# Batch 0's first values as floats over SyncE, cast by ScalarE

## The chip, the cores and the metric

The kernel runs on one core of one Trainium2 chip. Five engines work beside each other, each through its own instructions in program order, and wait for each other by semaphores: TensorE (PE), VectorE (DVE), ScalarE (ACT), GpSimd (POOL) and SyncE (SP). Sixteen DMA engines move data between the chip's main memory and its on-chip memory. DMAs are issued from SP and ACT on hardware queues (q1 in the profile is SP's) and from POOL on a software queue (q0). A DMA from POOL can change float32 to bfloat16 on its way; here those from SP carry the values as they are.

The metric is the device time of one execution, in microseconds (us), as the median of several runs.

## The reference

Two chained attentions feed a two-layer network. The 8 batches have 8 heads each, with 576 rows of 64 for q, k and v, and 32 "packing" rows p:

```python
def sm_attn(qq, kk, vv):
    s = scale * np.matmul(qq, kk.transpose(0, 1, 3, 2))
    s = s - np.max(s, axis=-1, keepdims=True)
    a = np.exp(s)
    a = a / (np.sum(a, axis=-1, keepdims=True) + 1e-09)
    return np.matmul(a, vv)
p_packed = sm_attn(p, k, v)
out = sm_attn(q, p_packed, p_packed)
```

The result, as 4608 rows of 512, goes through `h = x @ w_in` (512 by 2048), `g = relu(h) ** 2` and `g @ w_out` (2048 by 512). All inputs and the output are float32; the kernel computes in bfloat16 with float32 sums.

## The kernel before

**Order.** All instructions are issued by the class `Kernel` from one long string, `ORDER` (line 48). Each word is one step, `step` (line 780) turns it into a call, and a suffix names the engine (`:a` ACT, `:v` DVE, `:p` POOL). Nothing reorders the steps: every engine does its share of the words in the order of the string. The semaphore waits between engines come from the tiles that the steps write and read. So the place of a word decides what stands behind it on its engine.

**Work.** Heads are taken in "quads" of four (`QH`), two quads to a batch. For each batch the kernel loads k (`Lk`), v (`Lv`) and q (`Lq`, or `LA` and `LB` for two pieces), computes the first attention (scores `s1`, maximum `m1`, exponential `x1`, turning `eT` and its copy `eo`, product with the values `pv`), normalizes (`rd`, `pp`), and then the second attention from `zA`/`zB` or `s2` on. The second attention's weights are not multiplied with the packed values on their own: `w0` to `w3` multiply the packed values into `w_in`, so that layer 1 (`h`, then `r` for the relu and `q` for the square) works from the attention weights. Layer 2 is `o`, and `c` and `d` copy and store its rows. Digits after a word are batch and quad, or tile numbers. While batch 0's attention runs, there is nothing else for PE but `Z` words: matmuls on zeros (`busy`, line 337) whose result is not used.

**The start.** These words begin the string:

```python
pf Lk00 P0 Lk01 kT00 Z14.0 s100 Lv00 LA0 kT01 m100 Z1.1 s101 m101 I x100 Lv01 x101 P1 Z2.1 eT00 LB0 eo00:v Z0.1 eT01
```

- `pf` (`p_first`, line 226) issues three DMAs on SP: batch 0's p and the first quad of batch 1 (96 KB), then the rest in two pieces (24 KB and 8 KB). They land as floats in `p_f`, a corner of the tile `gT` that is not yet in use.
- `P0` (`p_cast`, line 232) has DVE scale and cast the two quads of batch 0 (line 235) and transpose them to `pT` (line 239). `P1` does so for batch 1. The scores need `pT`.
- `Lk00` and `Lk01` (line 297 on) load the two quads of keys from POOL, `Lv00` and `Lv01` (`load_v`, line 305) the two quads of values, `LA0` and `LB0` the queries, `Wi` pieces of `w_in`. They all share POOL's queue, in the order of the words. `I` makes the identity matrix on POOL.
- `kT00` and `kT01` (`st_k`, line 354) have DVE transpose the keys when they have landed. `s100` and `s101` (line 411) are the scores on PE, `Z14.0` fourteen fillers ahead of them and `Z1.1` two between them.
- `m100`, `m101` are DVE's maxima, `x100`, `x101` ACT's exponentials (line 451). They are ACT's first work.

For batches 0 and 1 a quad of values lies as 96 partitions by 4 heads by 6 rows of 64 in bfloat16, in a row of `gT` for each quad that is not yet in use; batch 0's first quad lies in row 14 and batch 1's quads in rows 12 and 11. `pv` (line 488) reads it from there, about 12 us into the span.

A DMA's packets are the contiguous rows that it moves: a quad of keys has 128 rows of 18 x 64 floats, a quad of values 96 x 4 rows of 6 x 64 floats, the first load of p 128 x 3 rows of 64 floats.

Of the kernel before, what the change touches and what calls it, by code (L numbers as in the profile page):

```python
# [11 lines left out]
F32 = mybir.dt.float32  # L12
# [9 lines left out]
D = 64  # L22
NP = 32
T = 18
S = T * NP
HALF = S // 2
QH = 4
# [18 lines left out]


ORDER = """
pf Lk00 P0 Lk01 kT00 Z14.0 s100 Lv00 LA0 kT01 m100 Z1.1 s101 m101 I x100 Lv01 x101 P1 Z2.1 eT00 LB0 eo00:v Z0.1 eT01
QA01 QA00 eo01:v Wi01 EA00:a rd0 pv0 pp0 EA01:a Z1.0 pt0 Wi00 po0:v Z0.1 zA0 tA00 Wi11 tA01 mA00 Z1.0 QB01 QB00 EB00:a  # L50
EB01:a mA01 sA00:v Wi10 Wi20 Z2.1 zB0 sA01:v xA00 xA01 tB00 Z5.0 w00 tB01 Wi21 mB00 W001:a Z3.0 w10 uA01 uA00 mB01
sB00:p aA01:p xB00 W000:a TA01 sB01:v aA00:p TA00 Lk11 uB00 W100:a h0.0.2 h0.0.3 Lk10 h0.0.0 xB01 h0.0.1 W101:a r0.0.3:a
# [82 lines left out]
class Kernel:  # L135
# [83 lines left out]
    def bank(self, pool, name):  # L219

        return self.banks(pool).tile([P, 512], F32, name=name, tag="t")

    def packed(self, g0, g1):
        return self.p.rearrange("b (q h) i d -> (h i) (b q) d", h=QH)[:, g0:g1, :]

# [65 lines left out]
    def load1(self, b, qd, n):  # L291
# [10 lines left out]
        else:  # L302
            self.load_rows(x, s, qd if b else 0)

    def load_v(self, t, s, b, qd):

        if b in THREES:
            c = b * S
            x = self.gT[:, self.NFB - 2 - 2 * b - qd, c:c + QH * 6 * D].rearrange("p (h j d) -> p h j d", h=QH, d=D)[:S // 6]
            t["v"] = [x[:, :, j, :] for j in range(6)]  # L310
            self.nc.gpsimd.dma_start(x, s.rearrange("h (p j) d -> p h j d", j=6))
            return
        x = self.v_b[self.loaded_v % len(self.v_b)]
        self.loaded_v += 1
        y = self.v_end[b % len(self.v_end)]
        t["v"] = [x[:, :, j, :] for j in range(4)]
        t["v_end"] = y
        o, r = (D, 0) if qd else (0, 4 * P)
        self.nc.gpsimd.dma_start(x, s[:, o:o + 4 * P].rearrange("h (p j) d -> p h j d", j=4))  # L319
        self.nc.gpsimd.dma_start(y[qd * D:(qd + 1) * D, :, qd, :], s[:, r:r + D].rearrange("h p d -> p h d"))  # L320
# [459 lines left out]
    def step(self, word):  # L780
        word, _, e = word.partition(":")
        engine = self.engines.get(e, self.nc.vector)
        q4 = self.NFB // 4
        if word == "I":
            make_identity(self.nc, self.ident)
        elif word == "pf":
            self.p_first()
        elif word in ("Pr", "Px", "Pt", "Pu"):
            self.p_rest(word, engine)
        elif word in ("P0", "P1"):  # L790
            self.p_cast(int(word[1]))
        elif word[0] == "Z":
            self.busy(*map(int, word[1:].split(".")))
        elif word[:2] == "Wi":
            self.load_w_in(int(word[2]), int(word[3]))
        elif word[:2] == "Wo":
            self.load_w_out(int(word[2]) * q4, (int(word[2]) + 1) * q4)
        elif word[:2] in ("w0", "w1", "w2", "w3"):
            self.st_wp(int(word[2]), int(word[1]))
        elif word[:2] in ("W0", "W1", "W2", "W3"):  # L800
            self.st_wp_out(int(word[2]), int(word[1]), engine, *map(int, word[3:]))
        elif word[:2] in ("s1", "s2", "zA", "zB", "rd", "pv", "pp", "bd", "bs", "pt", "po"):
            self.step_quads(word[:2], engine, int(word[2]), *([int(word[3])] if len(word) > 3 else range(self.NQ)))
        elif word[0] == "L" and len(word) == 3:
            self.load_q(int(word[2]), {"q": None, "A": 0, "B": 1}[word[1]])
        elif word[0] == "L":
            self.load1(int(word[2]), int(word[3]), word[1])
        elif "." in word or word[0] in "cd":
            {"H": self.step_hh, "R": self.step_rr, "h": self.step_h, "r": self.step_r, "q": self.step_q, "o": self.step_o, "c": self.step_c, "d": self.step_d}[word[0]](
                engine, *map(int, word[1:].split(".")))  # L810
        else:
            self.step_att(word[:-2], engine, int(word[-2]), int(word[-1]))
# [56 lines left out]
```

## Time and profile before

| | before |
|---|---|
| time, median of 3 runs | 240.65 us (240.53 to 240.82) |
| profiled execution | 240.85 us |
| its span, first to last instruction | 239.1 us |
| PE busy | 230.8 us, 97% of the span |
| DVE busy | 200.4 us, 84% |
| ACT busy | 143.9 us, 60% |
| POOL busy | 73.0 us, 31% |
| chain that ended last | PE 92%, DVE 5%, ACT 1% |
| POOL's queue q0 | 25312 packets, 18.55 MB, 53.7% of 16 engines' span |
| SP's queue q1 | 6384 packets, 9.51 MB, 14.9% |

How to read it: busy times count instructions that compute; the issue of a DMA and semaphore waits are not counted for PE, DVE and ACT. The chain that ended last is followed back from the last instruction to what released each step, so it says which engine's work set the end. "Idle before" in a row is the time for which the engine stood still just before an instruction, and behind the arrow is what ended that. The lines of the DMA queues give packets, megabytes and the time that the packets took as a share of all 16 engines over the stretch asked for; packets that overlap in time count twice, so shares over 100% occur. Megabytes are those written: a cast load reads twice as many.

### The profile page before, as it was taken

To read this page: it belongs to the slowest core of one execution; us is meant where nothing else is said; L and a number is where in the kernel's file an instruction comes from. 1 tells how busy PE (TensorE), PEld (TensorE's weight loads), DVE (VectorE), ACT (ScalarE), POOL (GpSimd) and SP (SyncE) were. 2 spreads that over 40 slices of the span, in tenths; PEclk is the share of its full clock that TensorE was granted. 3 is DMA by queue.
4 is the path that set the end of the run, shared out by engine and by line. 5 is a ranking of instruction groups with operands and counts; after the bars stand their busy time and mean duration, and the time that the engine had idled before them with its cause. 6 is when DMAs were issued, how large, how long until landed. Compare 5 with 4: busy or idle time off the path is not lost.

```text
span 239.1 us, 5971 instructions
## 1 busy us (share of the span) xinstructions
PE 230.8 (97%) x2355; PEld 123.5 (52%) x2355; DVE 200.4 (84%) x455; ACT 143.9 (60%) x311; POOL 73.0 (31%) x122
## 2 busy tenths in 40 slices
PE   8887999999999999999999999999999999999994
PEld 2444553456544564456545654565545644555543
DVE  2779986998997889989998889997899789987740
ACT  2348974887896657775683648774485346732300
POOL 8509782785664661054203340002000000000000
PEclk9999999999999999999999999999999999999999
DMA  6999999999999979169923993216112112111224
GB/s 109 193 200 213 200 206 204 161 243 211 199 203 217 192 106 143 44 91 197 127 64 45 195 129 60 47 44 96 45 27 67 47 44 46 44 47 44 49 59 111
DMA packets 31868, 28.50 MB, mean 119 GB/s; under 512 B 8161, under 2 KB 26337, under 8 KB 31841
## 3 DMA queue, kind: packets, MB, share of 16 engines
q0 software_dynamic: 25312, 18.55, 53.7%
q1 hardware_dynamic: 6384, 9.51, 14.9%
q8 instruction: 18, 0.29, 0.5%
q10 hardware_dynamic: 144, 0.07, 0.1%
q14 instruction: 10, 0.07, 0.1%
HBM read 37.22 MB, written 9.44 MB: 195 GB/s over the span
## 4 chain that ended last, share of the span: by engine, by line
PE 92%; DVE 5%; ACT 1%; issue 0%; ACTq 0%
PE ps_o L694 52%; PE ps_h L637 26%; PE ps_s L411 3%; PE ps_wp L623 3%; PE ps_idle L341 3%; PE ps_e1T L474 2%; PE ps_pv L507 1%; DVE r L644 1%; DVE sums L591 1%; ACT qT L457 1%; DVE wp L459 0%; PE ps_pv L500 0%; DVE a2T L613 0%; DVE gT L682 0%; DVE s L563 0%; PE ps_o L699 0%
## 5 line engine op out<-in xcount | busy, mean ns | idle before, releaser
L694 PE MATMUL ps_o<-w_out_bf,gT 128*128 128x512 bf16 (+1 forms) x576 | 147.0, 378 | 0.0
L637 PE MATMUL ps_h<-a2T,wp 128*128 128x288 bf16 (+2 forms) x512 | 89.9, 286 | 1.5 <-ACT wp L457 0.7
L642 ACT ACTIVATE r<-ps_h 128x288 bf16<-128x288 f32 (+2 forms) x161 | 61.4, 413 | 48.7 <-PE ps_h L637 44.0
L694 PEld LDWEIGHTS <-gT 128*128 128x128 bf16 x576 | 54.5, 98 | 43.9 <-issue 3.4
L637 PEld LDWEIGHTS <-wp 128*128 128x128 bf16 x512 | 47.5, 98 | 42.8 <-issue 7.7
L644 DVE TENSOR_SCALAR r<-ps_h 128x288 bf16<-128x288 f32 (+2 forms) x95 | 41.3, 449 | 11.8 <-PE ps_h L637 10.7
L682 DVE TENSOR_TENSOR gT<-r 128x576 bf16<-128x576 bf16 (+2 forms) x108 | 46.5, 444 | 2.3 <-ACT r L642 1.4
L457 ACT CAST wp<-ps_wp 128x1024 bf16<-128x1024 f32 (+1 forms) x31 | 29.2, 961 | 9.1 <-PE ps_wp L623 9.1
L457 ACT COPY o_sb<-ps_o 128x512 f32<-128x512 f32 x26 | 15.2, 590 | 12.3 <-PE ps_o L694 12.0
L271 POOL DMA_DIRECT2D q_b<-in_q_dram x16 | 10.9, 685 | 29.1 <-DVE qT L369 25.2
L319 POOL DMA_DIRECT2D v_b<-in_v_dram x12 | 9.3, 779 | 32.3 <-PE ps_pv L507 30.4
L271 POOL DMA_DIRECT2D k_b<-in_k_dram x28 | 15.3, 550 | 12.1 <-DVE kT L357 5.0
L451 ACT ACTIVATE e<-ps_s,nm 128x576 bf16<-128x576 f32 x16 | 11.8, 743 | 7.1 <-DVE nm L437 7.1
L357 DVE STREAM_TRANSPOSE kT<-k_b 128x576 uint32<-128x576 uint32 x16 | 12.3, 770 | 2.9 <-DMA k_b<-in_k_dram 2.9
L341 PE MATMUL ps_idle<-gT 128*128 128x512 bf16 (+1 forms) x34 | 11.4, 465 | 1.2 <-DVE gT L190 1.2
L437 DVE TENSOR_REDUCE nm<-ps_s 128x1 f32<-128x576 f32 x16 | 11.5, 740 | 1.1 <-PE ps_s L411 1.1
L369 DVE STREAM_TRANSPOSE qT<-q_b 128x576 uint32<-128x576 uint32 (+2 forms) x16 | 10.8, 683 | 2.0 <-DMA q_b<-in_q_dram 2.0
L680 ACT ACTIVATE gT<-r 128x640 bf16<-128x640 bf16 (+1 forms) x18 | 12.2, 694 | 0.4 <-DVE r L644 0.2
L591 DVE TENSOR_REDUCE sums<-e 128x18 f32<-128x576 f32 (+2 forms) x20 | 12.1, 604 | 0.0
L585 ACT ACTIVATE e<-d 128x576 f32<-128x576 f32 (+2 forms) x20 | 11.7, 600 | 0.6 <-DVE d L579 0.6
L579 DVE TENSOR_TENSOR d<-s,mx 128x576 f32<-128x576 f32 (+2 forms) x19 | 11.7, 641 | 0.0
L573 DVE TENSOR_REDUCE mx<-s 128x18 f32<-128x576 f32 (+2 forms) x20 | 11.6, 609 | 0.0
(68 smaller groups left out, 175.5 us busy)
## 6 DMA issues: line engine op xcount, KB each, us to landing
out_dram<-o_sb SPq DMA_DIRECT2D x65, 128.0 KB, 2.4
v_b<-in_v_dram POOLq DMA_DIRECT2D x12, 256.0 KB, 5.6
w_out_bf<-in_moe_w_out_dram POOLq DMA_DIRECT2D x4, 512.0 KB, 10.7
q_b<-in_q_dram POOLq DMA_DIRECT2D x6, 288.0 KB, 6.2
q_b<-in_q_dram POOLq DMA_DIRECT2D x12, 144.0 KB, 6.9
k_b<-in_k_dram POOLq DMA_DIRECT2D x12, 108.0 KB, 4.7
gT<-in_v_dram POOLq DMA_DIRECT2D x4, 288.0 KB, 7.9
w_in_bf<-in_moe_w_in_dram POOLq DMA_DIRECT2D x4, 256.0 KB, 10.7
```

Source lines behind the costliest of these rows:

```text
L271: engine.dma_start(x[n:], s[:P - n])
L341: self.nc.tensor.matmul(ps[:, :m], lhsT=self.nought[:, :P], rhs=self.nought[:, :m], start=True, stop=True)
L357: self.nc.vector.transpose(t["kT"][:].rearrange("p s e -> p (s e)").bitcast(U32), t["k"][:].rearrange("p t d -> p (t d)").bitcast(U32))
L451: self.nc.scalar.activation(out, x, ACT.Exp, bias=t["nm"], accum_out=self.den[b][:, qd:qd + 1])
L457: engine.copy(out, x)
L591: nc.vector.reduce_sum(out=sums[:, x], in_=t["e2"][:, x], axis=AX.X)
L637: self.nc.tensor.matmul(ps, lhsT=self.att[b, 0]["wp"][:, qd, fb * P:(fb + 1) * P], rhs=self.att[b, qd]["a2T"][:, s0:s1], start=(qd == 0), ...
L642: engine.activation(r, ps, ACT.Relu)
L644: engine.tensor_scalar_max(r, ps, 0.0)
L680: engine.activation(out, r, ACT.Square)
L682: engine.tensor_tensor(out=out, in0=r, in1=r, op=ALU.mult)
L694: self.nc.tensor.matmul(self.o[tt][:, e], lhsT=self.gT[:, fb, a:a + P], rhs=self.w_out_bf[:, fb, e], start=(i == 0), stop=(i == self.NFB - 1))
```

## The change

Batch 0's first quad of values no longer comes by a casting DMA of POOL. A new first word, `vf`, issues it on SP ahead of the three DMAs of p, as floats, into a corner of `gT` (96 partitions of rows 9 to 12, columns of batch 1) that nothing has used by then. `Lv00` is taken out of the order, so POOL's queue has one load less. A new word `vc:a`, between `I` and `x100`, has ACT cast the floats to the place in `gT` where `Lv00` put them. Everything after that is as before. `v_rows` only gives a name to the place.

```diff
-pf Lk00 P0 Lk01 kT00 Z14.0 s100 Lv00 LA0 kT01 m100 Z1.1 s101 m101 I x100 Lv01 x101 P1 Z2.1 eT00 LB0 eo00:v Z0.1 eT01
+vf pf Lk00 P0 Lk01 kT00 Z14.0 s100 LA0 kT01 m100 Z1.1 s101 m101 I vc:a x100 Lv01 x101 P1 Z2.1 eT00 LB0 eo00:v Z0.1 eT01
...
+    def v_first(self):
+
+        self.v_f = self.gT[:S // 6, 9:9 + QH, S:S + 12 * D].bitcast(F32).rearrange("p h (j d) -> p h j d", d=D)
+        self.nc.sync.dma_start(self.v_f, self.v[0, :QH].rearrange("h (p j) d -> p h j d", j=6))
+
+    def v_cast(self, engine):
+        x = self.v_rows(0, 0)
+        self.att.setdefault((0, 0), {})["v"] = [x[:, :, j, :] for j in range(6)]
+        self.copy(engine, x, self.v_f)
...
+    def v_rows(self, b, qd):
+
+        c = b * S
+        return self.gT[:, self.NFB - 2 - 2 * b - qd, c:c + QH * 6 * D].rearrange("p (h j d) -> p h j d", h=QH, d=D)[:S // 6]
...
         if b in THREES:
-            c = b * S
-            x = self.gT[:, self.NFB - 2 - 2 * b - qd, c:c + QH * 6 * D].rearrange("p (h j d) -> p h j d", h=QH, d=D)[:S // 6]
+            x = self.v_rows(b, qd)
             t["v"] = [x[:, :, j, :] for j in range(6)]
             self.nc.gpsimd.dma_start(x, s.rearrange("h (p j) d -> p h j d", j=6))
...
+        elif word == "vf":
+            self.v_first()
+        elif word == "vc":
+            self.v_cast(engine)
```

## The prediction

> **What bounds the kernel now.** I read PE's waits first, then busy times by stretch, then the first 9 us in order of time, then the DMA queues in short windows. First the longest and the last of PE's waits (engine, line, what it waited for: us in total, times, longest), then stretches of the span (length, then busy us of PE, PEld, DVE, ACT, POOL):
>
> ```profile
> PE ps_h L637 <- ACT wp L457: 0.7, 1, 0.7
> PE ps_h L637 <- DVE wp L459: 0.6, 1, 0.6
> ...
> PE ps_wp L623 <- DVE mx L573: 0.5, 1, 0.5
> ```
>
> ```profile
> 26.00:28.00 2.00, 1.60 (x14) 1.28 (x14) 2.00 (x4) 2.00 (x7) 0.89 (x2) 1.00 1.25 209
> 28.00:30.00 2.00, 2.00 (x60) 1.49 (x59) 1.83 (x5) 1.96 (x7) 1.38 (x2) 1.00 1.29 200
> 30.00:40.00 10.00, 9.97 (x145) 4.83 (x143) 7.07 (x20) 6.68 (x12) 5.85 (x9) 1.00 1.24 206
> 40.00:80.00 40.00, 40.00 (x396) 20.25 (x386) 35.95 (x83) 30.50 (x61) 25.59 (x43) 1.00 1.24 202
> 80.00:200.00 120.00, 120.00 (x1270) 65.14 (x1271) 109.63 (x242) 76.07 (x169) 22.76 (x38) 1.00 0.51 87
> ```
>
> ```profile
> 26.40 1.85 PE L637 MATMUL ps_h<-a2T,wp 128*128 128x256 bf16 x14 [0.58 <-DVE wp L459]
> ```
>
> The wait on DVE's wp ends at 26.4 us and is PE's last. From 28 us PE has no gap to speak of, so whatever delays PE before 28 us is added to the end, and a transfer that arrives sooner after 28 us buys nothing. The change is therefore priced in the front, where batch 0's attention runs as one chain over PE, DVE and ACT. Its start, in order of time (start us, us, engine, line, operation):
>
> ```profile
> 0.74 1.28 ACT L451 ACT_TABLE_LOAD   x1 [0.74 <-PEq L853]
> 0.74 0.46 SPq L229 DMA_DIRECT2D gT<-in_p_dram  x1
> ...
> 1.19 6.05 PE L341 MATMUL ps_idle<-gT 128*128 128x512 bf16 x14 [1.19 <-DVE gT L190]
> 1.24 1.25 POOL L271 DMA_DIRECT2D k_b<-in_k_dram  x2 [0.80 <-POOLq L853]
> ...
> 1.77 0.43 SPq L273 DMA_DIRECT2D gT<-in_p_dram  x1
> ...
> 2.48 0.69 POOL L311 DMA_DIRECT2D gT<-in_v_dram  x1
> ...
> 2.90 0.33 DVE L235 TENSOR_SCALAR p_b<-gT 128x128 bf16<-128x128 f32 x1 [1.21 <-DMA gT<-in_p_dram]
> 3.15 0.73 POOL L271 DMA_DIRECT2D q_b<-in_q_dram  x1
> 3.26 0.24 DVE L239 STREAM_TRANSPOSE pT<-p_b 128x64 uint32<-128x64 uint32 x1
> ...
> 5.73 0.78 DVE L357 STREAM_TRANSPOSE kT<-k_b 128x576 uint32<-128x576 uint32 x1 [2.23 <-DMA k_b<-in_k_dram]
> ...
> 7.16 0.78 DVE L357 STREAM_TRANSPOSE kT<-k_b 128x576 uint32<-128x576 uint32 x1 [0.65 <-DMA k_b<-in_k_dram]
> ...
> 7.17 0.69 PE L411 MATMUL ps_s<-kT,pT 32*32 32x192 bf16 x24
> ...
> 7.80 0.50 PE L341 MATMUL ps_idle<-gT 128*128 128x512 bf16 x2
> ...
> 8.23 0.69 PE L411 MATMUL ps_s<-kT,pT 32*32 32x192 bf16 x24
> 8.71 0.74 ACT L451 ACTIVATE e<-ps_s,nm 128x576 bf16<-128x576 f32 x1 [6.69 <-DVE nm L437]
> ```
>
> DVE works in program order: cast of p (P0) and its transpose, 2.90 to 3.50 (0.60 us); first key transpose when k_b lands at 5.73; second at 7.16. The first scores start at 7.17, held by PE's 14 filler matmuls until 7.24, though their kT was ready at 6.51. The second scores start at 8.23 behind two more fillers, though their kT was ready at 7.94. So there is slack: 0.66 us for the first k_b, 0.28 us for the second, and p may land as late as 7.17 - 0.78 - 0.60 = 5.79 us instead of 2.90.
>
> **The change, part by part.** These rows price the transfers. Queue rows are packets, MB, share of 16 engines; in order they are from the windows 1.8:2.6 (q1: SyncE's p), 2.6:3.5 and 3.5:5.5 (q0: GpSimd's k), 7:8 (q0: values), 8.6:9.6 (q0: values and queries), 50:51 (both queues), 205:205.4 (q1: outputs alone). Then issues with KB and us to landing, of the first 40 us, of the whole span, of 50:51.
>
> ```profile
> q1 hardware_dynamic: 485, 0.12, 64.8%
> ...
> q0 software_dynamic: 25, 0.06, 82.3%
> ...
> q0 software_dynamic: 175, 0.37, 101.4%
> ...
> q0 software_dynamic: 255, 0.19, 127.9%
> ...
> q0 software_dynamic: 222, 0.20, 122.8%
> ...
> q0 software_dynamic: 105, 0.09, 65.4%
> q1 hardware_dynamic: 122, 0.19, 53.5%
> ...
> q1 hardware_dynamic: 45, 0.09, 100.6%
> ```
>
> ```profile
> gT<-in_p_dram SPq DMA_DIRECT2D x1, 96.0 KB, 2.1
> ...
> gT<-in_p_dram SPq DMA_DIRECT2D x1, 8.0 KB, 4.1
> ...
> out_dram<-o_sb SPq DMA_DIRECT2D x65, 128.0 KB, 2.4
> ...
> out_dram<-o_sb SPq DMA_DIRECT2D x2, 128.0 KB, 5.6
> ```
>
> Time per packet is 16 engines x window x share / packets. A p packet: 16 x 0.8 x 0.648 / 485 = 17 ns. A k packet: 16 x 2 x 1.014 / 175 = 185 ns. A packet of today's values, which reads the same 1536 bytes the new load will read: 16 x 1 x 1.279 / 255 = 80 ns busy, 16 / 255 = 63 ns if only elapsed time counts. Query packets from 8.6 on: 16 / 222 = 72 ns elapsed.
>
> *The new load (vf).* 96 partitions x 4 heads = 384 packets, 24 on each engine. Its cost as floats isn't in the trace. Below: 63 ns. Above: outputs alone take 16 x 0.4 x 1.006 / 45 = 143 ns per 2048 bytes, so 107 ns for 1536. I take 80, because that row reads the same bytes from the same tensor. So 24 x 0.08 = 1.9 us of all engines, and it goes ahead of p on SyncE's queue and beside k. The three issues of p move back by one issue, 0.46 us, which is nothing beside the packets.
>
> *How the two queues share an engine.* At 50:51, with both queues full, 105 packets of the one went beside 122 of the other: about one for one. I take one for one. The small p load says the same of a late comer: 8 KB took 4.1 us where 96 KB ahead of it took 2.1, and outputs beside a full q0 took 5.6 against 2.4.
>
> *The sum, per engine.* q1 starts at 1.9 us (0.74 issue, first packets of p in the window from 1.8). Until q0 starts at 2.6: 0.7 / 0.08 = 9 packets of v. From 2.6 to 3.5 q0 only manages 25 / 16 = 1.6 packets (0.3 us); v fills the rest with 0.6 / 0.08 = 7.6. Then 7.6 of v and 14.4 of k are left. They alternate: 7.6 x (0.185 + 0.080) = 2.0 us, to 5.5. Now p's first load, 24 packets per engine, takes its turns: with the last 6.8 of k, 6.8 x (0.185 + 0.017) = 1.4, to 6.9; then with queries, 17.2 x (0.072 + 0.017) = 1.5, to 8.4. Today the 24 packets from 1.9 end at 2.3 and DVE starts at 2.90, so 0.55 us more: p lands at 9.0.
> DVE then needs 0.60 for P0 and 0.78 for the first kT, so the first scores start at 10.4 instead of 7.17: **+3.2 us**. The same account gives the last k packet at 6.9 instead of 3.5 + 14.4 x 0.185 = 6.2, so k lands 0.7 late; that is hidden behind p. The second scores follow the first by 1.06 as now.
>
> *The cast (vc:a) on ACT.* ACT's casts by shape (us busy, mean ns):
>
> ```profile
> L457 ACT CAST wp<-ps_wp 128x1024 bf16<-128x1024 f32 x27 | 26.9, 1018 | 7.6 <-PE ps_wp L623 7.6
> L457 ACT CAST wp<-ps_wp 128x512 bf16<-128x512 f32 x4 | 2.3, 579 | 1.5 <-PE ps_wp L623 1.5
> ```
>
> (1018 - 579) / 512 = 0.86 ns per element, so 1536 elements take 1018 + 439 = 1.46 us. The added wait is for v, landed by 5.5 + 0.5. Behind it on ACT stand the two exponentials, for which PE's transposes wait; the first runs at 8.71 now, so a v landed by 7.25 costs nothing even without the shift. The table load stays ahead, at 0.74. Nought; without that cover, 1.46.
>
> *GpSimd's queue.* One issue of 0.69 us goes, so the queries go out at 2.5 instead of 3.15, and the rest moves up. Two later weight loads wait for earlier landings, and PEld once for a weight:
>
> ```profile
> 9.16 0.61 POOL L259 DMA_DIRECT2D w_in_bf<-in_moe_w_in_dram  x1 [0.87 <-DMA gT<-in_v_dram]
> ...
> 10.61 0.61 POOL L259 DMA_DIRECT2D w_in_bf<-in_moe_w_in_dram  x1 [0.83 <-DMA q_b<-in_q_dram]
> ```
>
> ```profile
> PEld L623 <- DMA w_in_bf<-in_moe_w_in_dram: 1.0, 1, 1.0
> ```
>
> ```profile
> 19.25 0.41 PE L623 MATMUL ps_wp<-w_in_bf,ppT 64*32 64x512 bf16 x8 [0.55 <-DVE mx L573]
> ```
>
> The eleventh load waits for the third (values), the twelfth for the fourth (queries): eight are out at a time. With one gone they wait for the second k and the queries instead. The weight wait before 19.25 would go, but PE itself waited only 0.5 us there, for DVE's mx, which moves with the shift: nought. Bounds: a gain of 0.5, or, if w_in comes late, a loss of what the shift hasn't covered; with the front 3.2 us late it is covered.
>
> Sum: 240.85 (the profiled execution; its span is 239.1) + 3.2 = 244.05. That execution is 0.2 above the median of the runs shown, so 243.9.
>
> **The rivals.**
> *k, not p, is late.* If an engine sends p's small packets many at a time, p lands right behind v, before 5.8, and costs nothing. All that work still stands ahead of k: v 24 x 0.08 + p 0.6 + k 16 x 0.185 = 5.5 us from 1.9 is 7.4 instead of 6.2. The second k_b then lands 1.2 later, less 0.28 of slack: +0.9, 241.6; with 63 to 107 ns, 241.1 to 242.2. The 50:51 row speaks against it, but its packets are 2048 bytes, not 256.
> [...]
> *PE's clock.* The 14 fillers of 512 columns took 6.05 / 14 = 432 ns each; four of the same width later take 0.86 us on the chain:
>
> ```profile
> 30.19 0.86 PE ps_o L694 x4
> ```
>
> So PE starts at half rate, though the clock column of the stretches reads 1.00 there too. A pause from 7.24 to 10.4 may bring that back. Scores, fillers and scores (0.69 + 0.50 + 0.69) would then take between nothing and 1.9 us more; I take the middle, 1.0: 244.9.
> [...]
> *The transfer is hidden.* v fills only the hole before 3.5, p by 5.79 and the second k by 7.44: no change, 240.65 to 240.9. It needs small packets sent many at a time, and v well under 63 ns.
> *Faster.* With p and k in time as above, the sooner weights take away PE's 0.5 us before 19.25: 240.1. It decides only if p lands by 5.79, and DVE's mx isn't what holds PE there; the row names DVE, against it.
>
> **How the numbers follow.** p late 0.40: with v at 63 ns the same account ends at 8.3 instead of 9.0, with 107 at 9.9, so its own range is 243.1 to 244.8. p late with a slow PE 0.10, up to 244.8 + 1.9 = 246.7, k late 0.24, hidden 0.10, faster 0.16. Slower: 0.40 + 0.10 + 0.24 = 0.74; within 0.2% (0.5 us, about what a measurement of this kernel can tell from no change) 0.10; faster 0.16. The predicted time is the first case's, 243.9. The range 240.6 to 246.2 takes in the slower cases but for the last end and most of the hidden one, and leaves out the faster.
>
> **What would show it.** Right: DVE's P0 waits for gT<-in_p_dram until about 9, both kT follow it without a wait for k_b, the first scores start near 10.4, and PE is full from about 31 us. k late: P0 before 5.8, second kT near 8.4. Wrong altogether: the first scores near 7.2. The cast should take near 1.46 us and end before the first exponential; if ACT waits for v past m100, the added wait is on the path. Not to be seen is a new wait of PE after 31 us.

## The result: slower by 2.5 us, and the profile after

The changed kernel took 243.13 us (242.25 to 243.42, 4 runs) against 240.59 for the kernel before beside it: a ratio of 1.0100, with a 95% interval of 1.0072 to 1.0127. Measured twice more beside the experiments, on two other chips, it took 242.35 (ratio 1.0052, 1.0023 to 1.0081) and 242.57 (1.0065, 1.0046 to 1.0085). So it is slower each time, by 1.5 to 2.5 us.

The profiled execution took 243.42 us, its span is 241.6, against 240.85 and 239.1 before. Its start in order of time (start us, us, engine, line, operation; in brackets how long the engine had waited and for what):

```profile
0.74 0.39 SPq L226 DMA_DIRECT2D gT<-in_v_dram  x1
1.19 0.47 SPq L239 DMA_DIRECT2D gT<-in_p_dram  x1
...
1.25 1.25 POOL L281 DMA_DIRECT2D k_b<-in_k_dram  x2 [0.80 <-POOLq L871]
...
6.16 1.47 ACT L471 CAST gT<-gT 96x1536 bf16<-96x1536 f32 x1 [4.14 <-DMA gT<-in_v_dram]
6.36 0.23 DVE L245 TENSOR_SCALAR p_b<-gT 128x128 bf16<-128x128 f32 x1 [4.67 <-DMA gT<-in_p_dram]
...
7.44 0.78 DVE L371 STREAM_TRANSPOSE kT<-k_b 128x576 uint32<-128x576 uint32 x1 [0.58 <-DMA k_b<-in_k_dram]
...
8.28 0.69 PE L425 MATMUL ps_s<-kT,pT 32*32 32x192 bf16 x24 [1.25 <-DVE kT L371]
...
9.18 0.78 DVE L371 STREAM_TRANSPOSE kT<-k_b 128x576 uint32<-128x576 uint32 x1 [0.96 <-DMA k_b<-in_k_dram]
9.44 0.61 POOL L269 DMA_DIRECT2D w_in_bf<-in_moe_w_in_dram  x1 [1.12 <-DMA k_b<-in_k_dram]
10.01 1.15 PE L425 MATMUL ps_s<-kT,pT 32*32 32x192 bf16 x24 [0.62 <-DVE kT L371]
...
14.32 0.55 PE L521 MATMUL ps_pv<-gT,e1T 96*32 96x64 bf16 x48 [0.20 <-DVE e1T L473]
...
28.90 1.85 PE L651 MATMUL ps_h<-a2T,wp 128*128 128x256 bf16 x14 [0.58 <-DVE wp L473]
```

Before the change the product with the values stood here:

```profile
11.83 0.55 PE L507 MATMUL ps_pv<-gT,e1T 96*32 96x64 bf16 x48 [0.20 <-DVE e1T L459]
```

The positions p are there at 6.36, later than the 2.90 of before, but the first key transpose after them still waits 0.58 us for its keys, and the second 0.96. So the keys hold the front, not p. The second transpose starts at 9.18 instead of 7.16 (+2.0), the second scores at 10.01 instead of 8.23 (+1.8). From there another 0.7 us is lost on PE, whose second scores take 1.15 us instead of 0.69; the product with the values starts at 14.32 instead of 11.83 (+2.5). The last row is the one that ended PE's last wait in the profile before: 28.90 instead of 26.40, again +2.5, and +2.5 is the difference of the spans. Nothing is gained or lost after it.

TensorE in the stretches from 10 to 14 us, before and then after the change (length, then busy us of PE, PEld, DVE, ACT, POOL, then the granted clock, DMA share, GB/s):

```profile
10.00:12.00 2.00, 1.40 (x43) 1.09 (x44) 1.32 (x4) 0.93 (x3) 0.61 (x1) 1.00 1.24 205
12.00:14.00 2.00, 1.49 (x69) 0.79 (x55) 0.72 (x3) 0.74 (x2) 0.00 (x0) 1.00 1.18 185
```

```profile
10.00:12.00 2.00, 1.77 (x26) 1.13 (x27) 1.40 (x3) 0.83 (x3) 0.66 (x2) 0.50 1.23 208
12.00:14.00 2.00, 2.00 (x22) 1.87 (x21) 1.18 (x4) 0.83 (x2) 0.00 (x0) 0.65 1.15 176
```

The clock, 1.00 before the change in all stretches, is down to half for 3.4 us, from 9.97 to 13.39.

The DMA queues show why the keys are late. q1 is SyncE's queue (values, then p), q0 GpSimd's (keys); in order the windows 1.8:2.6, 2.6:3.5 and 3.5:5.5, as packets, MB, share of 16 engines:

```profile
q1 hardware_dynamic: 76, 0.12, 63.7%
...
q1 hardware_dynamic: 173, 0.27, 92.3%
...
q1 hardware_dynamic: 537, 0.30, 65.9%
q0 software_dynamic: 84, 0.19, 50.4%
```

From 2.6 to 3.5 no key packet went at all (25 before), and from 3.5 to 5.5 there were 84 instead of 175, although the keys were issued at the same 1.25 us.

### The profile page after: what moved, and what is told of

It is laid out like the page before. It is cut to its first block, busy times and chain, and to the rows that moved or that the text cites. A ratio compares the mean times of both kernels' runs of the same rounds, so it can differ in the third digit from the quotient of the medians.

```text
span 241.6 us, 5941 instructions
## 1 busy us (share of the span) xinstructions
PE 228.6 (95%) x2320; PEld 124.8 (52%) x2355; DVE 200.2 (83%) x455; ACT 145.4 (60%) x312; POOL 72.3 (30%) x121
## 4 chain that ended last, share of the span: by engine, by line
PE 86%; DVE 7%; DMA 3%; issue 2%; ACT 1%; POOL 0%; ACTq 0%; POOLq 0%
PE ps_o L708 49%; PE ps_h L651 25%; DMA k_b<-in_k_dram 3%; PE ps_wp L637 3%; PE ps_s L425 3%; PE ps_e1T L488 2%; PE ps_pv L521 1%; DVE gT L696 1%; DVE mx L587 1%; DVE d L593 1%; DVE r L658 1%; PE ps_idle L355 1%; DVE sums L605 1%; ACT qT L471 1%; DVE wp L473 0%
## 5 line engine op out<-in xcount | busy, mean ns | idle before, releaser
L708 PE MATMUL ps_o<-w_out_bf,gT 128*128 128x512 bf16 (+1 forms) x544 | 140.7, 378 | 2.0 <-issue 0.5
```

The lines of the kernel that those rows point to most:

```text
L708: self.nc.tensor.matmul(self.o[tt][:, e], lhsT=self.gT[:, fb, a:a + P], rhs=self.w_out_bf[:, fb, e], start=(i == 0), stop=(i == self.NFB - 1))
```

## The experiments

Every experiment was run beside the kernel before on the same chip. This table holds the steps of the front in the profiled execution of each (start of the second key transpose, of the second scores, of the product with the values, of the ps_h row that starts at 26.40 before, and the span), then the median time and the ratio to before with its interval.

| | 2nd kT | 2nd scores | pv | ps_h | span | median | ratio (95%) |
|---|---|---|---|---|---|---|---|
| before | 7.16 | 8.23 | 11.83 | 26.40 | 239.1 | | |
| changed | 9.18 | 10.01 | 14.32 | 28.90 | 241.6 | 243.13 | 1.0100 (1.0072 to 1.0127) |
| changed, second chip | 8.17 | 9.00 | 12.60 | 27.18 | 240.9 | 242.35 | 1.0052 (1.0023 to 1.0081) |
| changed, third chip | 8.95 | 9.93 | 13.99 | 28.56 | 241.2 | 242.57 | 1.0065 (1.0046 to 1.0085) |
| p on ScalarE's queue | 8.58 | 9.41 | 13.01 | 27.58 | 240.9 | 242.74 | 1.0084 (1.0059 to 1.0109) |
| p first | 7.56 | 8.39 | 15.34 | 30.06 | 243.0 | 245.27 | 1.0178 (1.0126 to 1.0229) |
| p first, cast late | 7.63 | 8.46 | 12.23 | 26.82 | 239.8 | 241.38 | 1.0029 (1.0010 to 1.0048) |
| load only | 8.08 | 8.91 | 12.50 | 27.31 | 240.0 | 241.96 | 1.0051 (1.0026 to 1.0077) |
| half | 8.80 | 9.64 | 13.23 | 27.80 | 240.7 | 242.64 | 1.0064 (1.0036 to 1.0092) |
| half, again | 8.89 | 9.72 | 13.32 | 27.89 | 241.9 | 243.04 | 1.0081 (1.0052 to 1.0110) |
| double | | 14.12 | 18.20 | 32.77 | 245.2 | 246.98 | 1.0259 (1.0243 to 1.0276) |
| more fillers | 8.26 | 9.51 | 13.11 | 27.69 | 240.6 | 242.56 | 1.0063 (1.0040 to 1.0087) |
| before, cold PE | 7.21 | 8.24 | 12.70 | 27.27 | 239.8 | 241.58 | 1.0022 (1.0003 to 1.0042) |
| w_out early | 8.91 | 9.74 | 13.33 | 27.92 | 241.3 | 243.06 | 1.0093 (1.0077 to 1.0108) |

**Is it p or the keys?** The three loads of p are issued on ScalarE's queue instead of behind the values on SyncE's:

```diff
-        self.nc.sync.dma_start(self.p_f[:, :n - 1, :], self.packed(0, n - 1))
+        self.nc.scalar.dma_start(self.p_f[:, :n - 1, :], self.packed(0, n - 1))
```

> The changed kernel with the three loads of p issued on ScalarE's hardware queue, so that p no longer stands behind the values; the values still go first on SyncE. Theory P (p late): P0 near 4, time back to about 240.6. Theory K: p is early, but the keys still wait for the values, the first kT near 7.4 and the second near 9.2, time 243.1 within 0.4.

```profile
0.75 0.48 ACTq L239 DMA_DIRECT2D gT<-in_p_dram  x1
...
5.87 0.23 DVE L245 TENSOR_SCALAR p_b<-gT 128x128 bf16<-128x128 f32 x1 [4.19 <-DMA gT<-in_p_dram]
...
8.58 0.78 DVE L371 STREAM_TRANSPOSE kT<-k_b 128x576 uint32<-128x576 uint32 x1 [0.62 <-DMA k_b<-in_k_dram]
```

p has a queue of its own and is issued as early as before, and still the time is 242.74 and the keys are waited for. The theory of p falls, that of the keys holds. P0 started only at 5.87 even so, against 2.90 before the change: the values held up a queue beside theirs as well.

**Where do the values stand?** First the order on SyncE alone is turned round, then the cast is moved as well:

```diff
-vf pf Lk00 P0 Lk01 kT00 ... I vc:a x100
+pf vf Lk00 P0 Lk01 kT00 ... I vc:a x100
```

> The changed kernel with the values' load issued on SyncE after the three loads of p instead of before them. Theory K (the keys land late because the engines take up the values before the keys): the keys' first packets now come before most of the values, so the first kT starts near 5.8 to 6.2, the second near 7.4 to 8.0, the second scores near 8.3 to 8.9, no pause of PE is long enough to slow its clock, and the time is 240.6 to 241.4. Theory W (what counts is only the amount of work that the DMA engines have before the second keys are complete, in whatever order): the second kT still starts near 8.7, time 242 or more. Theory P (p was what came late): P0 is back at 2.9 and the time at 240.6.

```profile
2.24 0.42 SPq L226 DMA_DIRECT2D gT<-in_v_dram  x1
...
7.56 0.78 DVE L371 STREAM_TRANSPOSE kT<-k_b 128x576 uint32<-128x576 uint32 x1 [1.02 <-DMA k_b<-in_k_dram]
...
10.57 1.47 ACT L471 CAST gT<-gT 96x1536 bf16<-96x1536 f32 x1 [8.55 <-DMA gT<-in_v_dram]
11.95 0.73 ACT L465 ACTIVATE e<-ps_s,nm 128x576 bf16<-128x576 f32 x1
...
12.82 0.88 PE L488 MATMUL ps_e1T<-ident,e 128*96 128x128 bf16 x6 [3.09 <-ACT e L465]
```

The keys were on time but for 0.4 us, as expected; the time was 245.27 and not 241. The values, issued at 2.24 behind p, landed only at 10.57, and the cast stood on ScalarE ahead of the exponentials: the first one ran at 11.95 instead of 8.71, and PE waited 3.09 us for it.

```diff
-vf pf Lk00 ... I vc:a x100 ... QA01 QA00 eo01:v Wi01 EA00:a
+pf vf Lk00 ... I x100 ... QA01 QA00 eo01:v Wi01 vc:a EA00:a
```

> The changed kernel with the positions loaded ahead of the values on SyncE's queue, and ScalarE's cast moved behind the first exponentials (just before the exponential of the second batch's first group). Theory order on ScalarE (what the order positions first lost is the cast, which stood in front of the exponentials while the values landed late): keys on time (second kT about 7.5, second scores about 8.4), values land about 10.6, cast 10.6 to 12.1, first product with the values about 12.1 instead of 11.83, time 240.9 to 241.2. Theory amount (the extra bytes and the extra cast cost whatever their order): 242 or more.

```profile
7.63 0.78 DVE L371 STREAM_TRANSPOSE kT<-k_b 128x576 uint32<-128x576 uint32 x1 [1.25 <-DMA k_b<-in_k_dram]
...
10.72 1.46 ACT L471 CAST gT<-gT 96x1536 bf16<-96x1536 f32 x1
...
12.23 0.55 PE L521 MATMUL ps_pv<-gT,e1T 96*32 96x64 bf16 x48 [0.37 <-ACT gT L471]
```

With the cast behind the exponentials the loss is 0.5 us (241.38), close to the 240.9 to 241.2 expected. Nearly all that the order p first had lost was the cast's place. The same bytes as in the change, over the same queue, cost about a third of it when they come behind p (0.52 us, and 1.49 for the change on the same chip). So what costs most is not that they are moved but that they stand ahead of the keys.

**Is it the load or the cast?** The float load stays ahead, its data is not used, the values come over GpSimd as before, and there is no cast:

```diff
-vf pf Lk00 P0 Lk01 kT00 Z14.0 s100 LA0 kT01 m100 Z1.1 s101 m101 I vc:a x100
+vf pf Lk00 P0 Lk01 kT00 Z14.0 s100 Lv00 LA0 kT01 m100 Z1.1 s101 m101 I x100
```

> The changed kernel with the float load of the values kept first on SyncE's queue but its data unused: the values come by the casting load on GpSimd's queue behind the keys, as before, and there is no cast. Theory keys (the float load ahead of the keys is what costs): second kT about 9, time 243.0 plus or minus 0.4, as the change itself. Theory cast (ScalarE's cast or the order of the work that it changes costs): as before, 240.4 to 240.9. The result's work is whole; one load is added.

241.96 us, with an interval that begins at 1.0026 x 240.86 = 241.5: the cast's theory is out. The time lies below the 243.0 expected, since the second key transpose started at 8.08 and not near 9. But the changed kernel itself, run beside it, had 8.17 and 242.35:

> The changed kernel itself, on the chip of these runs, to set the others beside it: 243.1 plus or minus 0.4; second kT between 8.3 and 9.2; the granted clock falls to about 0.5 between 10 and 12 us in a part of the executions.

The load alone costs as much as the whole change, within their intervals.

**Half and double.** For half, two heads come as floats and two by the casting load, which stays on GpSimd's queue:

```diff
-        self.v_f = self.gT[:S // 6, 9:9 + QH, S:S + 12 * D].bitcast(F32).rearrange("p h (j d) -> p h j d", d=D)
+        self.v_f = self.gT[:S // 6, 9:9 + QH // 2, S:S + 12 * D].bitcast(F32).rearrange("p h (j d) -> p h j d", d=D)
```

> The changed kernel with only two of the four heads of values over SyncE as floats and cast by ScalarE; the other two heads come over GpSimd's queue as before the change. Theory K: half the packets in front of the keys, so the second keys land about 1.0 late instead of 2.0 and the time is about 241.3 to 241.6. If any early load on SyncE costs the same whatever its size: 243.1. If it is GpSimd's shorter queue that matters: also near 243.

The time was 242.64, more than proportion allows. It was run again with the whole beside it:

> Half of the change again (two of the four heads as floats and cast, two by the casting load), now beside the whole on one chip. Theory proportion: half of the keys' delay, second kT about 7.7, time half way between before and the changed kernel of this call. Theory floor (any delay of the front runs GpSimd's queue dry and w_out comes late): within 0.4 of the changed kernel, with the queue below 160 GB/s in the stretches from 24 to 28 us.

> The changed kernel itself, beside the next three on one chip: 242.4 plus or minus 0.5. The second kT between 8.1 and 9.2. If PE reaches the product with the values less than 1 us late, it waits for a weight of layer 2 (w_out) between 40 and 50 us.

Half took 243.04 and the whole 242.57: no proportion. In both profiles of half the second keys came as late as in the whole (8.80 and 8.89). Window 5:6, first half, then the whole on the same chip:

```profile
q0 software_dynamic: 50, 0.11, 78.3%
q1 hardware_dynamic: 34, 0.01, 4.9%
```

```profile
q0 software_dynamic: 85, 0.18, 98.8%
q1 hardware_dynamic: 82, 0.02, 9.8%
```

The keys did begin earlier in half: 63 packets from 3 to 4 us and 73 from 4 to 5, where the whole beside it has 1 and 40. But after 4.5 us the engines were not full while the keys came: 78.3% on q0 where the whole has 98.8%. What kept them from it was not found. The floor that the second theory puts on any delay was not shown either; GpSimd's queue did run thin here (130 GB/s from 26 to 28 us), but it had done that in the whole too, at another time (95 from 22 to 24). A part of half's time is not from the front at all: in its second profile the ps_h row is 1.5 us late and the span 2.8 longer. Of the other 1.3 the profile names a wait of PE of 0.27 us for the transposed queries at 41.78 and little else.

For double, a second load of the same size goes ahead of the first:

```diff
+        v_2 = self.gT[:S // 6, 5:5 + QH, S:S + 12 * D].bitcast(F32).rearrange("p h (j d) -> p h j d", d=D)
+        self.nc.sync.dma_start(v_2, self.v[0, QH:].rearrange("h (p j) d -> p h j d", j=6))
         self.nc.sync.dma_start(self.v_f, self.v[0, :QH].rearrange("h (p j) d -> p h j d", j=6))
```

> The changed kernel with a second float load of the same size (the second quad of values, not used) ahead of the first on SyncE's queue; the result's work is whole. Theory engines finish what SyncE queued before they take keys: 24 more packets of 0.065 us, so keys and positions 1.6 later than the changed kernel's of this call: second kT about 9.8, second scores about 10.6, time 243.6 to 244.6. Theory one for one (keys and values alternate from the start): the keys land near 7.2 as before, positions only at about 10, first scores above 11; time 244.5 to 245.5. Theory nothing in proportion (half cost as much as the whole): within 0.5 of the changed kernel.

```profile
8.99 0.62 POOL L271 DMA_DIRECT2D w_in_bf<-in_moe_w_in_dram  x1 [1.97 <-DMA k_b<-in_k_dram]
10.64 0.61 POOL L271 DMA_DIRECT2D w_in_bf<-in_moe_w_in_dram  x1 [1.03 <-DMA k_b<-in_k_dram]
11.08 0.23 DVE L247 TENSOR_SCALAR p_b<-gT 128x128 bf16<-128x128 f32 x1 [9.39 <-DMA gT<-in_p_dram]
...
12.29 1.15 PE L427 MATMUL ps_s<-kT,pT 32*32 32x192 bf16 x24 [5.17 <-DVE kT L373]
```

Its queues in the windows 5:6, 7:8 and 9:10:

```profile
q1 hardware_dynamic: 163, 0.25, 105.6%
q0 software_dynamic: 2, 0.00, 2.4%
...
q0 software_dynamic: 85, 0.19, 96.9%
q1 hardware_dynamic: 83, 0.02, 15.8%
...
q0 software_dynamic: 115, 0.16, 88.7%
q1 hardware_dynamic: 116, 0.03, 21.3%
```

246.98 us, more than any theory gave. GpSimd's wait for the second keys, at 9.21 in the whole beside it, ends at 10.64 (+1.4, for 1.6 expected), so the engines did finish the values first. But p, most of which had gone ahead of most of the keys in the change, now went beside them, packet for packet (85 to 83, 115 to 116), and landed at 11.08, after both. Each theory had half of it. The runs fit this reading: what SyncE's queue holds when the keys arrive goes first, up to some depth, and only what lies deeper alternates with them. PE then ran cold on top: its first scores took 1.15 us.

**TensorE's clock.** In the kernel before, the fillers ahead of the first scores are cut, so that PE arrives cold with the keys on time:

```diff
-pf Lk00 P0 Lk01 kT00 Z14.0 s100
+pf Lk00 P0 Lk01 kT00 Z0.1 s100
```

> The kernel before with the first batch's filler cut from 14.0 to 0.1 in the planned order, so that TensorE arrives cold at the scores while the keys land as before. Only the idle filler is left out; the result's work is whole. Theory clock (the slow TensorE after the pauses is a cost of its own): second scores end up to 0.3 us earlier than 8.23 begins them now, but the granted clock is 0.5 from about 7 to at least 10.4 us, and the time comes out at 241.1 to 241.4. Theory keys alone (only the late landing of the keys costs, the clock is hidden in the waits): 240.3 to 240.6.

```profile
6.41 1.15 PE L411 MATMUL ps_s<-kT,pT 32*32 32x192 bf16 x24 [4.82 <-DVE kT L357]
...
8.24 1.15 PE L411 MATMUL ps_s<-kT,pT 32*32 32x192 bf16 x24
...
12.70 0.55 PE L507 MATMUL ps_pv<-gT,e1T 96*32 96x64 bf16 x48
```

241.58, 0.7 us over before: a cold PE is a cost of its own, of about the size seen in the change. The second scores started no later than before (8.24 to 8.23), but took 1.15 us instead of 0.69, and the product with the values came 0.87 late. The other way round, fillers were added to the changed kernel until the pauses were gone:

```diff
-vf pf ... Z14.0 s100 LA0 kT01 m100 Z1.1 s101
+vf pf ... Z19.0 s100 LA0 kT01 m100 Z3.1 s101
```

> The changed kernel with five more fillers on PE ahead of the first scores and two more ahead of the second ones, so that PE does not pause while it waits for the keys. Theory C (of the loss of 2.5 us, 1.8 is the late keys and 0.7 the slower clock of PE after its pause): the granted clock stays at 1.00 from 10 to 14 us, the second scores still start near 10.0, and the time falls by 0.7 to 242.4. If the clock is only seen and costs nothing: 243.1 as the changed kernel. If the fillers themselves stand in the way: slower than 243.1.

242.56, as expected by the theory of the clock, and the mean granted clock was 0.998 or more in all ten runs, where the first four runs of the changed kernel had 0.993, 0.991, 1.0 and 0.993. It was not run beside the changed kernel, though, and that took as little on the two other chips. So the fillers are not shown to help. They also stand in the way a little: in this profile the second scores start 1.25 us after the second key transpose (9.51 after 8.26), behind four fillers, against 0.83 to 0.98 in the three profiles of the change.

**A second chain through GpSimd's queue?** In the second profile of the change the front is only 0.8 us late (27.18), but the span is 1.8 longer. The rest is one wait:

```profile
26.00:28.00 2.00, 1.42 (x11) 0.90 (x10) 2.00 (x3) 1.99 (x5) 1.67 (x2) 1.00 0.93 134
```

```profile
45.61 3.18 PE L708 MATMUL ps_o<-w_out_bf,gT 128*128 128x512 bf16 x14 [0.90 <-DMA w_out_bf<-in_moe_w_out_dram]
```

GpSimd issues the loads of the second phase only when its own work on the late chain is done; the earlier loads are through by then, the queue falls to 134 GB/s (209 before), and a weight of layer 2 comes late. So the first of these loads was issued earlier, at about 11 us:

```diff
-tB01 Wi21 mB00 W001:a ... uB01 Wo0 r0.0.2:a
+tB01 Wi21 Wo0 mB00 W001:a ... uB01 r0.0.2:a
```

> The changed kernel with the first load of w_out issued right behind the last load of w_in, so that GpSimd's queue has work between 22 and 28 us, where it ran dry with the change (123 to 134 GB/s in two stretches against 194 to 209 before). Theory second chain (a part of the loss is the dry queue, by which the weights of layer 2 come late): the stretches from 22 to 28 us are back at about 200 GB/s, no wait for w_out at 45 us, and the time is 0.5 to 0.9 below the changed kernel's of this call. Theory front alone (only the late keys and TensorE's clock count): the same as the changed kernel's within 0.3.

```profile
26.00:28.00 2.00, 1.42 (x22) 0.53 (x22) 1.87 (x3) 1.99 (x5) 1.82 (x2) 1.00 1.12 200
```

```profile
30.56 0.70 PE L425 MATMUL ps_s<-kT,pT 32*32 32x192 bf16 x48 [0.79 <-DVE kT L371]
```

The queue is full again and the wait for w_out is gone, but the time is 243.06, half a us above the changed kernel beside it (242.57; the intervals overlap). The next batch's keys now stand behind that weight and hold PE for 0.79 us at 30.56. So the gain expected didn't come: the wait moved. How much of the median is due to a dry queue stays open, as the other two profiles of the change show no such wait of PE.

No version run here beats the kernel before.

## Why the prediction was right in sign and near in time, and wrong in its mechanism

- *PE is full from 28 us, so the front sets the end.* Right in the profile of the change, to the tenth. Not always: the second profile had a wait of 0.90 at 45.61, which the prediction had ruled out, and in half, again, 1.3 us were lost behind the front.
- *The price of a packet of values.* Right. From 2.6 to 3.5 it is 16 x 0.9 x 0.923 / 173 = 77 ns, for the 80 taken.
- *"Until q0 starts at 2.6 ... 9 packets of v", and "v fills the rest" of the hole to 3.5.* Wrong at first: only 76 / 16 = 4.8 packets per engine went by 2.6. The slow start that the keys showed before now falls on the values, which read first.
- *"They alternate".* This is the step that failed. Once both queues are full, one for one is right: 85 key packets beside 82 of p in window 5:6 of the whole, and the counts of double. But the engines did not begin so. From 2.6 to 3.5 they sent 173 packets of SyncE's queue and none of the keys, and from 3.5 to 5.5 537 to 84. The values and most of p went ahead, and p was there at 6.36 and not at 9.0.
- *The keys 0.7 late and hidden behind p.* Wrong with it: they hold the front. This is the rival "k, not p, is late", which had a chance of 0.24. It priced the second keys at +1.2 and the front at +0.9. In the three profiles of the change the second transpose was 1.0, 1.8 and 2.0 late and the second scores 0.8, 1.7 and 1.8. The second profile is the rival as priced; the others are later by most of a us. The head start that the change showed: when the first packet of the keys went, at 4.17 us, 347 of the values' 384 packets were gone and 168 of p's; by 5.5 us all 384 and 373 of p's 512, beside 84 of the keys' 256.
- *PE's clock.* The second rival, put at 0 to 1.9 us with 1.0 in the middle, is true in part: 2.49 at the product with the values less 1.78 at the second scores is 0.7 in the first profile, 2.16 - 1.70 = 0.5 in the third and nothing in the second. The cold kernel before gives it as 0.7.
- *The cast.* 1.47 us measured for 1.46, and hidden: it ends at 7.63, and the first exponential runs at 10.63. "Without that cover, 1.46" was too low; with p first, where it stood ahead of the exponentials, its wait for the values counted as well.
- *GpSimd's queue.* Right: the waits of the weight loads moved to the keys and queries, and the 0.5 us gain did not come.
- *The sum.* 243.9 against 243.13 came near through two errors: 3.2 us for p that were not lost, and 1.8 for the keys and 0.7 for the clock that were. That they nearly cancel is luck.

## What to carry to other kernels

In these runs a transfer issued ahead of a critical one was not merely in competition with it, even on another queue: what is queued first may go out nearly whole before the later queue gets its first packet, as 347 of the values' 384 packets did here, so price it at its full length, not at its share. Spare time of the DMA engines at the very start is no gap to fill with a large load that isn't needed yet, which cost 1.5 to 2.5 us here; put what the first matmul needs first, and let the rest come behind. An engine's cast of data from a DMA belongs behind the work that doesn't need it, or a late landing stops the whole chain, as with p first, where PE waited 3.09 us.

## What the runs showed of the hardware

- The queue that came second waited. The keys, issued at 1.25 us each time, had no packet from 2.6 to 3.5 in the change, and in double only 2 between 5 and 6 us. When the values were issued at 2.24 behind p they landed only at 10.57, over 8 us after their issue. How deep the head start goes was not measured: in the change the values (24 packets per engine) had it nearly whole, and a part of p; in double, where the values alone were 48 per engine, p did not. The packets say the same: in the change the first of p went at 3.77 us and the first of the keys at 4.17, 0.40 later; in double 2 of the keys went between 5 and 6 us, with 1 packet under 512 bytes beside them, and p's 256-byte packets after that (48 under 512 bytes from 6 to 7).
- The first large read ran slowly in both kernels, by GpSimd's queue before and by SyncE's after: 25 packets of keys from 2.6 to 3.5 before, 76 of values from 1.8 to 2.6 after, which is 16 x 0.8 / 76 = 168 ns elapsed per packet, against 16 x 0.9 / 173 = 83 in the next window.
- The granted clock fell to 0.50 in the first profile of the change, after PE had stood still for 1.25 and 0.62 us between short work. The pause alone doesn't decide: the second profile had 1.66 us of it ahead of the first scores and kept its clock, the third 1.97 and lost it. PE's work in the 3.41 us just ahead sorts these three. Here are these stretches, of the first profile with the one behind it, then of the second:

```profile
6.56:9.97 3.41, 1.58 (x28) 0.74 (x27) 1.83 (x5) 1.07 (x1) 1.59 (x3) 1.00 1.21 201
9.97:13.39 3.42, 3.16 (x37) 2.44 (x38) 2.15 (x5) 1.66 (x4) 0.69 (x2) 0.50 1.19 191
```

```profile
4.27:7.68 3.41, 1.75 (x16) 0.74 (x18) 1.46 (x3) 1.47 (x1) 3.35 (x6) 1.00 1.14 211
```

The third profile had 1.46 us of work from 5.39 to 8.81 and half the clock from 8.81 to 12.22. With p first the clock was at half for 3.40 us, from 12.32 to 15.72, and in double for 6.84, from 10.16 to 17.00, both reckoned from its mean in stretches of 2 us (0.58 and 0.57; 0.54, 0.50, 0.50 and 0.75). In the 3.41 us ahead of these two falls PE had about 0.8 and 0.4 us of work, in the stretches shown 1.58 ahead of a fall and 1.75 where the clock stayed. The other profiled executions had a mean clock of 0.998 or more. That is seen, not set by a run.
- The cold PE of the kernel before without its fillers runs its scores in 1.15 instead of 0.69 us, and the clock column reads 1.00 all the same. The durations of the matmuls show it, the column doesn't: it reads 1.00 in every stretch from 0 to 16 us. It did so in the kernel before too, where the 14 fillers at the start took 432 ns each; the clock's first record in that trace stands at 7.01 us.
- The landing of the second keys differs by 1.0 us between three profiles of the same changed kernel (second transpose at 8.17, 8.95 and 9.18).
